# Value products in halves of 32 rows for four heads, and TensorE transposes for the first two batches, in a decay-attention and SiLU feed-forward kernel

## Chip, cores, metric

One core of a Trainium2 chip. The metric is device time in microseconds (us), the median of the fast runs. A span in a profile is that of one profiled run; it is 1.7 to 2.1 us shorter than the time of the same run. The engines are TensorE (PE; its weight loads are PEld), VectorE (DVE), ScalarE (ACT), GpSimd (POOL) and the sync engine (SP), which here only issues DMAs. The granted clock is the share of its full clock that TensorE was given; the DMA share is the mean busy share of the core's DMA engines.

## The reference

```python
def _attn_ref(q, k, v, f):                      # q, k, v: (8, 8, 576, 64), f: (8, 8, 576)
    scores = (1 / sqrt(64)) * (q @ k.T)
    cum = cumsum(log(clip(f, 1e-4, 1)))
    scores = scores + cum[..., :, None] - cum[..., None, :]      # causal: the rest is -1e9
    attn = softmax(scores)                                       # [the -max step is cut here]
    return attn @ v

x = attn_out.transpose(0, 2, 1, 3).reshape(4608, 512)            # the 8 heads of a token side by side
h = x @ w_in                                                     # w_in: 512 x 2048
return (h * sigmoid(h)) @ w_out                                  # w_out: 2048 x 512
```

All inputs are float32. The kernel computes in bf16 with float32 sums.

## The kernel before

The kernel takes two heads of one batch as a *unit* (4 units per batch, 32 in all). The decay factor of the row cancels between numerator and denominator, so only the key's factor `w` is left: it is multiplied into `v` (giving `vp`), and the denominator is the product of `w` with the same `u = exp(scores)`. The scores are computed transposed, keys on partitions, so q and k are needed with the head dimension on partitions. That is what the DMA transposes are for.

```python
def load_qk(n):                                # 128 rows of 64 floats: pieces of 256 bytes
    nc.sync.dma_start(out=t[:, :, i, :],
        in_=src[b, 2*p+i, 0:SM, :].rearrange("(c p) d -> p c d", p=P))
# ... cast_qk: GpSimd casts to bf16 ...
def transposes(n):                             # one DMA transpose per unit, on the sync queue
    nc.sync.dma_start_transpose(out=t, in_=qbf.pop(n))
# ... scores(n, c): four pieces per unit; ScalarE exp from PSUM to u; DVE masks ...

def den(qd):                                   # a quad = two units = four heads
    for kb, (q0, q1), j in ...:                # head j on partitions 32j .. 32j+31
        nc.tensor.matmul(dn[32*j : 32*j+32, q0:q1],
            lhsT=w_bf[:, kb, bh:bh+1].to_broadcast([P, 32]), rhs=u_part(...))
    nc.scalar.activation(out=rec, in_=dn, func=ACT.Copy)
def rec_part(qd, part):                        # half of the columns each
    nc.vector.reciprocal(out=rec[:, r], in_=rec[:, r])
    # after part 1: 8 DMAs copy each head's 32 rows twice, to the 64 partitions of its numerator
    nc.sync.dma_start(out=rb[i*D + 32*h : i*D + 32*h + 32, :], in_=rec[32*j : 32*j+32, :])
def num(n):                                    # a unit: two heads, 64 rows each
    nc.tensor.matmul(nm[i*D : (i+1)*D, q0:q1], lhsT=vp[:, kb, 2*p+i, :], rhs=u_part(...))
    nc.vector.tensor_tensor(out=xT[:, p, ...], in0=nm, in1=rb, op=ALU.mult)    # reads PSUM

def m1_chunk(g, fc):   # 4 matmuls 128x512 with w_in, tanh on ScalarE, gate on DVE -> gt
def m2_part(g, tb, part):  # 4 matmuls 128x512 with w_out; after the 4th part evict and store
def fill(n):           # n chunks of feed-forward, m1 or m2, from groups whose xT is finished
    ...
    if can1 and (not can2 or a - c <= 16 + (c % 2)): m1_chunk(...)
    else: m2_part(...)
def finished(n): ...   # counts the groups of 512 tokens whose xT is complete after unit n
# steady(n): scores in two pairs with fills between; den after each second unit,
# num of the pair one unit later
```

In before the sync queue stands up to 9.3 us at a copy with loads behind it. Two score-sized buffers of PSUM (`psc`) serve scores, denominators and numerators; four more (`pbig`) serve the feed-forward. There are 288 chunks of feed-forward.

The softmax here doesn't subtract the row's maximum and nothing guards it: scores larger than these inputs give would overflow.

## Time and profile before

| | before |
|---|---|
| time, median of 3 runs | 440.25 us (438.83 to 440.57) |
| span of the profiled run | 436.2 us |
| TensorE busy | 336.6 us (77%) |
| start of unit 8 (first of the third batch) | 106.4 us |
| from there to the end | 329.8 us |

Table of stretches of before. The columns are start:end and length; the busy time (instructions) of PE, PEld, DVE, ACT and POOL; the granted TensorE clock; the DMA share; and GB/s.

```profile
0.00:63.00 63.00, 17.63 (x215) 10.39 (x217) 18.83 (x35) 17.32 (x22) 20.16 (x42) 0.91 0.91 175
63.00:106.00 43.00, 25.21 (x225) 10.44 (x228) 23.42 (x40) 21.39 (x33) 12.93 (x19) 0.77 1.14 198
...
150.00:358.00 208.00, 187.02 (x1671) 88.32 (x1699) 138.45 (x220) 123.07 (x191) 53.55 (x84) 1.00 0.71 153
358.00:436.00 78.00, 73.85 (x365) 33.65 (x369) 25.18 (x37) 27.89 (x47) 0.00 (x0) 0.99 0.16 55
```

TensorE is busy for only 42.8 of the first 106 us, while the DMA share is at or above 0.9. The kernel has a bad start, and a steady part with about 10% of idle time.

Timeline of before in the start: start, length, engine, line, operation and count. In brackets is the idle time before the instruction and what ended it.

```profile
23.56 7.18 SPq L115 DMA_DIRECT2D vf_201<-in_v_dram  x1
30.79 4.43 SPq L115 DMA_DIRECT2D vf_202<-in_v_dram  x1
...
35.33 4.24 SPq L213 DMA_TRANSPOSE qkT<-qkb  x1
...
41.82 0.85 PE L238 MATMUL sc<-qkT 64*128 64x400 bf16 x6 [18.34 <-DMA qkT<-qkb]
...
43.31 5.04 SPq L303 DMA_DIRECT2D rb<-rec  x8
```

The sync queue is held up at value loads, and behind them stands the DMA transpose that the fourth unit's scores need. TensorE waits 18.34 us for it.

Who the sync queue waited for in before (total, times, longest):

```profile
SPq L380 <- ACT osb L379: 70.6, 14, 12.5
SPq L303 <- DVE rec L295: 53.7, 11, 9.3
```

The second line is the head of the queue standing still until a reciprocal is done. Every load and transpose behind it stands too. The table of TensorE's waits for 150 to 358 us in before shows what the steady part pays:

```profile
PE sc L238 <- DMA qkT<-qkb: 17.2, 12, 2.7
```

Three groups of the page of before (line, engine, operation, shape, count; busy us and mean ns; idle before and its releaser):

```profile
L325 DVE TENSOR_TENSOR xT<-nm,rb 128x576 bf16<-128x576 f32 x32 | 23.9, 756 | 52.3 <-DMA rb<-rec 33.7
...
L316 PE MATMUL nm<-u,vp 128*64 128x64 bf16 (+4 forms) x576 | 27.5, 252 | 3.3 <-DVE xT L325 2.4
...
L281 PE MATMUL dn<-u,w_bf 128*32 128x64 bf16 (+4 forms) x576 | 15.9, 256 | 1.3 <-DVE u L252 0.9
```

### The profile page before, as it was taken

How to read it: one execution, taken by the hardware profiler on the slowest of the kernel's cores; microseconds unless marked ns; L12 is line 12 of the kernel's file. 1: busy time of each engine (PE TensorE's matmuls, PEld its weight loads, DVE VectorE, ACT ScalarE, POOL GpSimd, SP SyncE). 2: the span in 40 equal slices, each digit the busy share in tenths (PEclk: the TensorE clock that was granted, in tenths of full speed). 3: DMA queues.
4: the chain of work that ended last, by engine and by line, in shares of the span. 5: the costliest groups of instructions: out<-in, count | busy, mean ns of one | idle time of the engine just before them, and what ended most of it. 6: DMA issues, size and time to landing. Idle time of an engine off the chain costs nothing.

```text
span 436.2 us, 7419 instructions
## 1 busy us (share of the span) xinstructions
PE 336.6 (77%) x2774; PEld 158.4 (36%) x2821; DVE 235.0 (54%) x375; ACT 213.2 (49%) x328; POOL 97.9 (22%) x163
## 2 busy tenths in 40 slices
PE   0511728608298899788988997898899899999996
PEld 0300403303143344344443443344444444444442
DVE  3230528616388438485847674776768472634310
ACT  3621208507266547465655555565667542543421
POOL 3424216403240144133213411350143000000000
PEclk9999859957789999999999999999999999999999
DMA  6999769899544987697598839894941413001011
GB/s 153 199 189 195 166 155 213 153 208 203 129 101 101 200 194 154 162 212 170 120 200 182 198 83 218 167 209 99 215 123 37 117 36 107 24 29 45 37 61 72
DMA packets 167092, 61.47 MB, mean 141 GB/s; under 512 B 154192, under 2 KB 158288, under 8 KB 167056
## 3 DMA queue, kind: packets, MB, share of 16 engines
q1 hardware_dynamic: 162832, 56.80, 61.2%
q0 software_dynamic: 4224, 4.19, 5.9%
q8 instruction: 22, 0.36, 0.4%
q14 instruction: 14, 0.11, 0.1%
HBM read 36.85 MB, written 9.44 MB: 106 GB/s over the span
## 4 chain that ended last, share of the span: by engine, by line
PE 42%; SPq 27%; DMA 18%; ACT 5%; issue 4%; DVE 2%; POOL 1%; POOLq 0%; DVEq 0%; ACTq 0%
PE hp L343 19%; PE po L370 18%; SPq L303 11%; DMA qkT<-qkb 11%; SPq L77 6%; SPq L115 5%; SPq L213 4%; DMA vf_199<-in_v_dram 3%; ACT u L245 3%; PE sc L238 3%; DMA rb<-rec 2%; PE nm L316 2%; ACT th L351 2%; PE dn L281 1%; DMA vf_3622<-in_v_dram 1%
## 5 line engine op out<-in xcount | busy, mean ns | idle before, releaser
L343 PE MATMUL hp<-xT,w_in_bf 128*128 128x512 bf16 x560 | 141.0, 390 | 10.4 <-DVE xT L325 8.0
L351 ACT ACTIVATE th<-hp 128x512 bf16<-128x512 f32 x144 | 85.4, 602 | 107.8 <-PE hp L343 107.7
L370 PE MATMUL po<-w_out_bf,gt 128*128 128x512 bf16 x545 | 132.5, 379 | 3.3 <-issue 2.5
L245 ACT ACTIVATE u<-sc 128x800 bf16<-128x800 f32 x128 | 100.0, 841 | 68.1 <-PE sc L238 67.8
L352 DVE SCALAR_TENSOR_TENSOR gt<-th,hp 128x512 bf16<-128x512 bf16 x144 | 94.6, 674 | 39.1 <-ACT th L351 38.3
L252 DVE TENSOR_TENSOR u<-u,mask 128x256 bf16<-128x256 bf16 x128 | 53.2, 431 | 74.2 <-ACT u L245 73.1
L238 PE MATMUL sc<-qkT 64*128 64x176 bf16 (+5 forms) x512 | 38.9, 269 | 70.2 <-DMA qkT<-qkb 63.5
L343 PEld LDWEIGHTS <-w_in_bf 128*128 128x128 bf16 x576 | 53.0, 99 | 73.4 <-issue 17.4
L370 PEld LDWEIGHTS <-gt 128*128 128x128 bf16 x576 | 53.8, 98 | 64.2 <-issue 2.6
L295 DVE RECIPROCAL rec<-rec 128x288 f32<-128x288 f32 x32 | 61.9, 1942 | 13.2 <-ACT rec L289 13.2
L99 POOL CAST qkb<-qf 128x512 bf16<-128x512 f32 x31 | 19.2, 619 | 198.1 <-DMA qkT<-qkb 122.9
L238 PEld LDWEIGHTS <-qkT 64*128 64x128 bf16 x512 | 20.1, 99 | 102.3 <-DMA qkT<-qkb 74.8
L325 DVE TENSOR_TENSOR xT<-nm,rb 128x576 bf16<-128x576 f32 x32 | 23.9, 756 | 52.3 <-DMA rb<-rec 33.7
L379 ACT ACTIVATE osb<-po 128x512 f32<-128x512 f32 x36 | 21.6, 601 | 25.3 <-PE po L370 24.8
L316 PE MATMUL nm<-u,vp 128*64 128x64 bf16 (+4 forms) x576 | 27.5, 252 | 3.3 <-DVE xT L325 2.4
L316 PEld LDWEIGHTS <-vp 128*64 128x64 bf16 x576 | 20.3, 115 | 14.9 <-issue 10.0
L99 POOL CAST qkb<-kf 128x512 bf16<-128x512 f32 x31 | 19.2, 619 | 2.4 <-DMA kf<-in_k_dram 2.3
L289 ACT ACTIVATE rec<-dn 128x576 f32<-128x576 f32 x16 | 10.4, 651 | 15.5 <-PE dn L281 13.4
L281 PE MATMUL dn<-u,w_bf 128*32 128x64 bf16 (+4 forms) x576 | 15.9, 256 | 1.3 <-DVE u L252 0.9
L281 PEld LDWEIGHTS <-w_bf 128*32 128x32 bf16 x576 | 10.6, 101 | 11.5 <-issue 7.1
L103 POOL CAST qkb<-qktf 128x128 bf16<-128x128 f32 x32 | 9.7, 303 | 5.5 <-DMA qktf<-in_k_dram 5.5
L257 DVE TENSOR_TENSOR u<-u,mask_t 128x128 bf16<-128x128 bf16 x32 | 7.6, 238 | 0.0
(69 smaller groups left out, 63.9 us busy)
## 6 DMA issues: line engine op xcount, KB each, us to landing
rb<-rec SPq DMA_DIRECT2D x128, 72.0 KB, 2.1
out_dram<-osb SPq DMA_DIRECT2D x36, 256.0 KB, 2.5
qf<-in_q_dram SPq DMA_DIRECT2D x64, 128.0 KB, 3.1
kf<-in_k_dram SPq DMA_DIRECT2D x64, 128.0 KB, 3.1
w_in_bf<-in_moe_w_in_dram POOLq DMA_DIRECT2D x4, 512.0 KB, 11.8
w_out_bf<-in_moe_w_out_dram POOLq DMA_DIRECT2D x4, 512.0 KB, 11.6
qktf<-in_q_dram SPq DMA_DIRECT2D x8, 128.0 KB, 3.2
qktf<-in_k_dram SPq DMA_DIRECT2D x8, 128.0 KB, 3.2
```

Source lines behind the costliest of these rows:

```text
L99: engs[i].tensor_copy(out=t2[:, c0 : c0 + NM, :], in_=t[:, :, :, :].rearrange("p c h d -> p c (h d)"),)
L238: nc.tensor.matmul(sc[:, i, lo - c * CW : hi - c * CW], lhsT=t[r, k_off(kb) : k_off(kb) + P], rhs=t[r, q0 : q0 + hi - lo], start=True, sto ...
L245: nc.scalar.activation(out=u[:, :, c * CW : (c + 1) * CW], in_=sc[:, :, 0:CW], func=ACT.Exp, scale=scale)
L252: nc.vector.tensor_tensor(out=x, in0=x, in1=mask[:, None, :].to_broadcast([P, 2, P]), op=ALU.mult)
L281: nc.tensor.matmul(dn[32 * j : 32 * j + 32, q0:q1], lhsT=w_bf[:, kb, bh : bh + 1].to_broadcast([P, 32]), rhs=u_part(n, i, kb, q0, q1), sta ...
L295: nc.vector.reciprocal(out=rec[:, r], in_=rec[:, r])
L303: nc.sync.dma_start(out=rb[i * D + 32 * h : i * D + 32 * h + 32, :], in_=rec[32 * j : 32 * j + 32, :],)
L316: nc.tensor.matmul(nm[i * D : (i + 1) * D, q0:q1], lhsT=vp[:, kb, 2 * p + i, :], rhs=u_part(n, i, kb, q0, q1), start=(kb == 0), stop=(kb = ...
L343: nc.tensor.matmul(hp[:, :], lhsT=w_in_bf[:, cc, fc * P : (fc + 1) * P], rhs=xT[:, cc, t0 : t0 + TG], start=(cc == 0), stop=(cc == NCC - 1),)
L351: nc.scalar.activation(out=th[:, :], in_=hp[:, :], func=ACT.Tanh, scale=0.5)
L352: nc.vector.scalar_tensor_tensor(out=gt[:, fc, :], in0=th[:, :], scalar=1.0, in1=hp[:, :], op0=ALU.add, op1=ALU.mult,)
L370: nc.tensor.matmul(po[:, :], lhsT=gt[:, fc, tb * P : (tb + 1) * P], rhs=w_out_bf[:, fc, :], start=(fc == 0), stop=(fc == NFC - 1),)
```

## The change

The intent has three parts.

- Products are made as two passes over four heads, 32 of the 64 value rows each, so a numerator lies on the same partitions as the denominator. No copies of the reciprocal are needed, and ScalarE can evict numerators before the reciprocal is there. The features of `xT` come out in another order, so the rows of `w_in` are loaded permuted to match.
- The first two batches are transposed by matmuls with the identity, so the start needs no DMA transpose, and their q and k are read in rows of 1 KB. The permuted token order is undone by a strided PSUM write.
- The schedule is written anew: all first loads up front, GpSimd for the multiplies, 16 feed-forward chunks in batch 1, and from the third batch on 7 and 11 fills in turn (9 per unit).

The diff, cut to its core:

```diff
 def load_qk(n):
+    if n < NPT:                                            # NPT = 8 units
+        nc.sync.dma_start(out=t[:, i*NM*D : (i+1)*NM*D],
+                          in_=s.rearrange("(p c) d -> p (c d)", p=P))
 def transposes(n):
+    if n >= NPT: ... DMA transpose as before; return
+    for x0 in (0, NM + 1):                                 # q, then k
+        for c in range(NM):
+            nc.tensor.matmul(tp[:, :, c], lhsT=src[:, x0 + c, :], rhs=ident_bf)
+        nc.vector.tensor_copy(out=t[:, x0 : x0 + NM, :], in_=tp)
+        # ... the tails likewise, between q and k ...
-        for m in range(2): ... 8 DMAs rb <- rec ...
-def num(n): ... 64 rows per head, DVE multiply from PSUM ...
+def quad(qd, what):                                        # what: half 0, half 1, or 2 = w
+    nc.tensor.matmul(dn[HD*j : HD*(j+1), q0:q1],
+        lhsT=w or vbf[b][:, kb, h, what*HD : (what+1)*HD], rhs=u_part(...))
+def num(qd, e):
+    nc.scalar.activation(out=nm, in_=quad(qd, e)[:, 0:S], func=ACT.Copy)
+def divide(qd, e, eng):
+    eng.tensor_tensor(out=xT[:, (2*qd % NP) + e, ...], in0=nm, in1=recs[qd], op=ALU.mult)
 # load_w_in: moe_w_in.rearrange("(g j e r) f -> g e j r f", j=4, e=2)
 # third batch on, in unit n:
+    scores(n, 0); scores(n, 1); fill(2)
+    # load_qk(n + 4); cast_qk(n + 2); transposes(n + 2); ...
+    fill(2); scores(n, 2); scores(n, 3); fill(3)
+    if n % 2 == 1:
+        fill(1); den(m); rec_part(m, 0); num(m, 0); num(m, 1); fill(1); rec_part(m, 1)
+        divide(m, 0, nc.gpsimd); divide(m, 1, nc.gpsimd); fill(2); finished(n)
```

More of the change, by code (lines that the diff above doesn't have):

```diff
@@ L43 @@
     NX = 2 * NM + 1
+    NPT = 2 * NP
+    NQ = NU // 2
+    HD = D // 2
     assert D == 64 and S == 576 and DM == H * D and NP == NCC
@@ L55 @@
     recp = ctx.enter_context(tc.tile_pool(name="recp", bufs=2))
-    rbp = ctx.enter_context(tc.tile_pool(name="rbp", bufs=4))
+    nmp = ctx.enter_context(tc.tile_pool(name="nmp", bufs=4))
     tpool = ctx.enter_context(tc.tile_pool(name="tpool", bufs=3))
@@ L74, in load_qk @@
         for name, src in (("qf", q), ("kf", k)):
-            t = stage.tile([P, NM, 2, D], FP32, name=name, tag=name, bufs=5)
+            t = stage.tile([P, 2 * NM * D], FP32, name=name, tag=name, bufs=4)
             for i in range(2):
-                nc.sync.dma_start(
-                    out=t[:, :, i, :],
-                    in_=src[b, 2 * p + i, 0:SM, :].rearrange("(c p) d -> p c d", p=P),
-                )
+                s = src[b, 2 * p + i, 0:SM, :]
+                if n < NPT:
+                    nc.sync.dma_start(
+                        out=t[:, i * NM * D : (i + 1) * NM * D],
+                        in_=s.rearrange("(p c) d -> p (c d)", p=P),
+                    )
+                else:
+                    nc.sync.dma_start(
+                        out=t[:, :].rearrange("p (c h d) -> p c h d", h=2, d=D)[:, :, i, :],
+                        in_=s.rearrange("(c p) d -> p c d", p=P),
+                    )
             ts.append(t)
@@ L98, in cast_qk @@
             c0 = i * (NM + 1)
-            engs[i].tensor_copy(
-                out=t2[:, c0 : c0 + NM, :],
-                in_=t[:, :, :, :].rearrange("p c h d -> p c (h d)"),
-            )
+            dst = t2[:, c0 : c0 + NM, :]
+            if n < NPT:
+                engs[i].tensor_copy(
+                    out=dst.rearrange("p c (h d) -> p c h d", h=2),
+                    in_=t[:, :].rearrange("p (h c d) -> p c h d", h=2, d=D),
+                )
+            else:
+                engs[i].tensor_copy(out=dst, in_=t[:, :].rearrange("p (c x) -> p c x", c=NM))
         nc.gpsimd.tensor_copy(
@@ L123 @@
     load_tails(0)
-    load_qk(1)
+    for n in range(1, NP):
+        load_qk(n)
+    for c in range(NM + 1):
+        load_v(0, c)
     ident_bf = const.tile([P, P], BF16, name="ident_bf")
@@ L140, with load_w_in @@
     w_bf = const.tile([P, NM + 1, BH], BF16, name="w_bf")
-    WQ = 4
-    def load_w_in(i):
-        c0, c1 = i * DFF // WQ, (i + 1) * DFF // WQ
-        nc.gpsimd.dma_start(
-            out=w_in_bf[:, :, c0:c1],
-            in_=moe_w_in[:, c0:c1].rearrange("(cc p) f -> p cc f", p=P),
-        )
+    w_in_v = moe_w_in.rearrange("(g j e r) f -> g e j r f", g=NCC // 2, j=4, e=2)
+    def load_w_in(i):
+        c0, c1 = i * DFF // 2, (i + 1) * DFF // 2
+        for cc in range(NCC):
+            nc.gpsimd.dma_start(
+                out=w_in_bf[:, cc, c0:c1], in_=w_in_v[cc // 2, cc % 2, :, :, c0:c1]
+            )
+    WQ = 4
     def load_w_out(i):
@@ L179, with weights, convert_v @@
     nc.vector.tensor_copy(out=wexp[:, S : S + ST], in_=wexp[:, SM:S])
-    wps = pbig.tile([P, NM + 1, BH], FP32, name="wps", tag="big")
-    for c in range(NM + 1):
-        nc.tensor.transpose(wps[:, c, :], wexp[:, c * P : (c + 1) * P], ident_f[:, :])
-    nc.vector.tensor_copy(out=w_bf[:, :, :], in_=wps[:, :, :])
-    setup_pool.__exit__(None, None, None)
-    gpool = ctx.enter_context(tc.tile_pool(name="gpool", bufs=2))
+    def weights():
+        wps = pbig.tile([P, NM + 1, BH], FP32, name="wps", tag="big")
+        for c in range(NM + 1):
+            nc.tensor.transpose(wps[:, c, :], wexp[:, c * P : (c + 1) * P], ident_f[:, :])
+        nc.vector.tensor_copy(out=w_bf[:, :, :], in_=wps[:, :, :])
     qkT: dict[int, bass.AP] = {}
     us: dict[int, tuple] = {}
-    def convert_v(b, c):
+    def convert_v(b, c, eng=nc.gpsimd):
         if b not in vbf:
@@ L197, in convert_v @@
             r = slice(ST, P)
-            nc.gpsimd.memset(vp[0:ST, NM, :, :], 0.0)
+            eng.memset(vp[0:ST, NM, :, :], 0.0)
         n = r.stop - r.start
-        nc.gpsimd.tensor_tensor(
+        eng.tensor_tensor(
             out=vp[r, c, :, :],
@@ L211, in transposes @@
     def transposes(n):
+        src = qbf.pop(n)
         t = qktp.tile([P, NX, P], BF16, name="qkT", tag="qkT")
-        nc.sync.dma_start_transpose(
-            out=t[:, :, :], in_=qbf.pop(n)[:, :, :].rearrange("p x c -> p (x c)")
-        )
         qkT[n] = t[:, :, :].rearrange("p x c -> p (x c)")
+        if n >= NPT:
+            nc.sync.dma_start_transpose(
+                out=t[:, :, :], in_=src[:, :, :].rearrange("p x c -> p (x c)")
+            )
+            return
+        for x0 in (0, NM + 1):
+            tp = pbig.tile([P, P, NM], FP32, name="tp", tag="big")
+            for c in range(NM):
+                nc.tensor.matmul(
+                    tp[:, :, c],
+                    lhsT=src[:, x0 + c, :],
+                    rhs=ident_bf[:, :],
+                    start=True,
+                    stop=True,
+                )
+            nc.vector.tensor_copy(
+                out=t[:, x0 : x0 + NM, :].rearrange("p x c -> p (x c)"),
+                in_=tp[:, :, :].rearrange("p t c -> p (t c)"),
+            )
+            if x0 == 0:
+                tt = pbig.tile([P, 8 * P], BF16, name="tt", tag="big")
+                nc.tensor.transpose(tt[:, 0:P], src[:, NM, :], ident_bf[:, :])
+                nc.vector.tensor_copy(out=t[:, NM, :], in_=tt[:, 0:P])
     UO = [0]
@@ L270 @@
     recs: dict[int, bass.AP] = {}
-    dens: dict[int, tuple] = {}
-    def den(qd):
+    def quad(qd, what):
+        b = qd * 2 // NP
         dn = psc.tile([P, 1024], FP32, name="dn", tag="sc")
@@ L278, in den @@
                     n, i = 2 * qd + j // 2, j % 2
-                    b, p = divmod(n, NP)
-                    bh = b * H + 2 * p + i
+                    h = 2 * (n % NP) + i
+                    if what == 2:
+                        w = w_bf[:, kb, b * H + h : b * H + h + 1].to_broadcast([P, HD])
+                    else:
+                        w = vbf[b][:, kb, h, what * HD : (what + 1) * HD]
                     nc.tensor.matmul(
-                        dn[32 * j : 32 * j + 32, q0:q1],
-                        lhsT=w_bf[:, kb, bh : bh + 1].to_broadcast([P, 32]),
+                        dn[HD * j : HD * (j + 1), q0:q1],
+                        lhsT=w,
                         rhs=u_part(n, i, kb, q0, q1),
@@ L287, in den @@
                     )
+        return dn
+    def den(qd):
+        dn = quad(qd, 2)
         rec = recp.tile([P, S], FP32, name="rec", tag="rec")
         nc.scalar.activation(out=rec[:, :], in_=dn[:, 0:S], func=ACT.Copy)
-        dens[qd] = rec
+        recs[qd] = rec
     def rec_part(qd, part):
-        rec = dens[qd]
         r = slice(part * S // 2, (part + 1) * S // 2)
-        nc.vector.reciprocal(out=rec[:, r], in_=rec[:, r])
-        if part == 0:
-            return
-        for m in range(2):
-            rb = rbp.tile([P, S], FP32, name="rb", tag="rb")
-            for i in range(2):
-                j = 2 * m + i
-                for h in range(2):
-                    nc.sync.dma_start(
-                        out=rb[i * D + 32 * h : i * D + 32 * h + 32, :],
-                        in_=rec[32 * j : 32 * j + 32, :],
-                    )
-            recs[2 * qd + m] = rb
-    def num(n):
-        b, p = divmod(n, NP)
-        vp = vbf[b]
-        nm = psc.tile([P, 1024], FP32, name="nm", tag="sc")
-        for kb in range(NM + 1):
-            for q0, q1 in q_parts(kb):
-                for i in range(2):
-                    nc.tensor.matmul(
-                        nm[i * D : (i + 1) * D, q0:q1],
-                        lhsT=vp[:, kb, 2 * p + i, :],
-                        rhs=u_part(n, i, kb, q0, q1),
-                        start=(kb == 0),
-                        stop=(kb == NM or (kb == NM - 1 and q0 < SM)),
-                    )
-        us.pop(n)
-        rb = recs.pop(n)
-        nc.vector.tensor_tensor(
-            out=xT[:, p, b * S : (b + 1) * S], in0=nm[:, 0:S], in1=rb[:, :], op=ALU.mult
+        nc.vector.reciprocal(out=recs[qd][:, r], in_=recs[qd][:, r])
+    nms: dict[tuple, bass.AP] = {}
+    def num(qd, e):
+        dn = quad(qd, e)
+        nm = nmp.tile([P, S], FP32, name="nm", tag="nm")
+        nc.scalar.activation(out=nm[:, :], in_=dn[:, 0:S], func=ACT.Copy)
+        nms[qd, e] = nm
+    def divide(qd, e, eng):
+        b = qd * 2 // NP
+        eng.tensor_tensor(
+            out=xT[:, (2 * qd % NP) + e, b * S : (b + 1) * S],
+            in0=nms.pop((qd, e))[:, :],
+            in1=recs[qd][:, :],
+            op=ALU.mult,
         )
@@ L382 @@
     done = {"m1": 0, "m2": 0}
-    ready = {"g": 0}
+    ready = {"g": 0, "m2": False}
     def fill(n):
@@ L388, in fill @@
             can1 = a < 16 * ready["g"] and a < 16 * (c // 16) + 32
-            can2 = c < 16 * (a // 16) and a >= 32
+            can2 = c < 16 * (a // 16) and ready["m2"]
             if not can1 and not can2:
@@ L402, in finished @@
             ready["g"] += 1
+    POOLS = (nc.gpsimd, nc.gpsimd)
     transposes(0)
-    for n in range(1, NP):
-        load_qk(n + 1)
-        cast_qk(n, (nc.gpsimd, nc.gpsimd))
-        if n == NP - 1:
-            for c in range(NM + 1):
-                load_v(0, c)
-        transposes(n)
-    for i in range(WQ):
-        load_w_in(i)
-    for c in range(NM + 1):
-        convert_v(0, c)
-    load_tails(1)
-    load_qk(NP + 1)
-    def steady(n):
+    weights()
+    setup_pool.__exit__(None, None, None)
@@ new lines @@
+    gpool = ctx.enter_context(tc.tile_pool(name="gpool", bufs=2))
+    for n in range(NP):
+        scores(n, 0)
+        scores(n, 1)
+        if n + 1 < NP:
+            cast_qk(n + 1, POOLS)
+            transposes(n + 1)
+        scores(n, 2)
+        scores(n, 3)
+        if n == 1:
+            den(0)
+            load_qk(NP)
+            load_tails(1)
+            load_qk(NP + 1)
+        if n == 2:
+            rec_part(0, 0)
+            rec_part(0, 1)
+            for c in range(NM + 1):
+                convert_v(0, c, nc.gpsimd if c < 2 else nc.vector)
+            load_w_in(0)
+            load_w_in(1)
@@ new lines @@
+    den(1)
+    rec_part(1, 0)
+    rec_part(1, 1)
+    for m in range(2):
+        for e in range(2):
+            num(m, e)
+            divide(m, e, nc.gpsimd if m == 0 else nc.vector)
+    finished(NP - 1)
+    load_qk(NP + 2)
+    load_qk(NP + 3)
+    for c in range(NM + 1):
+        load_v(1, c)
+    cast_qk(NP, POOLS)
+    fill(3)
+    transposes(NP)
+    fill(1)
+    for n in range(NP, 2 * NP):
+        scores(n, 0)
+        scores(n, 1)
+        if n + 1 < 2 * NP:
+            cast_qk(n + 1, POOLS)
+            transposes(n + 1)
+        load_qk(n + NP)
+        if n == NP:
+            load_tails(2)
+        fill(1)
+        scores(n, 2)
+        scores(n, 3)
+        fill(1)
+        if n % 2 == 1:
+            m = n // 2
+            if n == NP + 1:
+                for c in range(NM + 1):
+                    convert_v(1, c)
+            den(m)
+            rec_part(m, 0)
+            rec_part(m, 1)
+            for e in range(2):
+                num(m, e)
+                divide(m, e, nc.gpsimd)
+            fill(2)
+            if n == NP + 1:
+                for i in range(WQ):
+                    load_w_out(i)
@@ L421, in steady @@
+    finished(2 * NP - 1)
+    for c in range(NM + 1):
+        load_v(2, c)
+    for n in (2 * NP, 2 * NP + 1):
+        cast_qk(n, POOLS)
+        transposes(n)
+    ready["m2"] = True
+    for n in range(2 * NP, NU):
         b, p = divmod(n, NP)
@@ L423, in steady @@
         scores(n, 1)
-        fill(1)
-        if n + 2 < NU and n + 2 >= NP:
-            cast_qk(n + 2, (nc.gpsimd, nc.gpsimd))
-        if n + 5 < NU and n >= NP:
-            load_qk(n + 5)
-        if b + 1 < B:
-            if p == 0 and b > 0:
-                load_tails(b + 1)
-            if p == 2 and b > 0:
-                for c in range(NM + 1):
-                    load_v(b + 1, c)
-        if b > 0:
-            if p == 0:
-                for c in range(2):
-                    convert_v(b, c)
-            if p == 1:
-                for c in range(2, NM + 1):
-                    convert_v(b, c)
@@ L442, in steady @@
-        if n == NP + 2:
-            for i in range(WQ):
-                load_w_out(i)
-        fill(1 if n >= 2 * NP else 0)
+        fill(2)
+        if n + 4 < NU:
+            load_qk(n + 4)
+        if n + 2 < NU:
+            cast_qk(n + 2, POOLS)
+            transposes(n + 2)
+        if p == 0 and b + 1 < B:
+            load_tails(b + 1)
+        if p < 2:
+            for c in range(2 * p, 2 + 3 * p):
+                convert_v(b, c)
+        if p == 1 and b + 1 < B:
+            for c in range(NM + 1):
+                load_v(b + 1, c)
@@ L446, in steady @@
+        fill(2)
         scores(n, 2)
         scores(n, 3)
-        fill(4 - n % 2 if n >= 2 * NP else 1)
+        fill(3)
         if n % 2 == 1:
-            den(n // 2)
-            rec_part(n // 2, 0)
-            fill(2 if n >= 2 * NP else 1)
-            rec_part(n // 2, 1)
-            fill(1 if n >= 2 * NP else 0)
-            if n == NP - 1:
-                for m in range(NP):
-                    num(m)
-                finished(n)
-                fill(4)
-        elif n >= 2 and n != 2 and n != NP:
-            num(n - 2)
-            num(n - 1)
-            fill(2 if n >= 2 * NP else 1)
-            finished(n - 1)
@@ L465, in steady @@
-        if n + 2 < NU and n + 2 >= NP:
-            transposes(n + 2)
-        if n + 5 < NU and 1 <= n < NP:
-            load_qk(n + 5)
-        if n == NP - 1:
-            for c in range(NM + 1):
-                load_v(1, c)
-    for n in range(NU):
-        steady(n)
-    fill(12)
-    num(NU - 2)
-    fill(2)
-    num(NU - 1)
-    finished(NU - 1)
+            m = n // 2
+            fill(1)
+            den(m)
+            rec_part(m, 0)
+            for e in range(2):
+                num(m, e)
@@ L480 @@
+            fill(1)
+            rec_part(m, 1)
+            for e in range(2):
+                divide(m, e, nc.gpsimd)
+            fill(2)
+            finished(n)
     while fill(1):
```

## The prediction

> **What bounds it now.** By the page, the span is 436.2 us, TensorE busy 336.6 (77%). At the tail's rate (8 matmuls of 128x512 in 1.73 us, chain of waits) the 1,152 feed-forward matmuls need 249 us; scores, denominators and value products add about 33 + 14 + 26: some 320 us. The other 115 are start and waits. By the table of stretches TensorE is busy 17.6 of the first 63 us, 25.2 of 63-106 (granted clock 0.77), 187 of 208 in 150-358, 74 of 78 in the tail.
>
> The start is lost to the sync queue and its DMAs. In the timeline the queue stands at value loads from 20.7 to 35 us (one lands after 13.4), a DMA transpose then takes 4.2 us to issue, and scores wait 18.3; later 8 copies rb<-rec per pair of units (5.0 us of issue), and the queue waits 53.7 us in total for the reciprocal before them. Feed-forward starts in earnest at 63 us; unit 8 (third batch) at 106.4. In 150-358 TensorE waits 17-24 us for DMA transposes.
>
> **What changes.**
> - Removed: 128 copies (9.4 MB, some 75 us of queue issue, and the wait before them).
> - TensorE stays level: four heads of 32 columns fill 128 columns as two of 64 did [...]. The trace agrees: a denominator pass (36 matmuls) takes 0.87 us, a pair of units' products 1.59. Two passes: 1.74; +2.4 us over 16.
> - ScalarE: 32 evictions of about 0.65 us, +21. DVE: most multiplies (0.76 us) leave for GpSimd, an estimated 1.2-1.3 us each from its 1.04-1.1 for 128x512. Neither becomes the limit.
> - First 8 units: 8 DMA transposes go; per unit TensorE gains 9 small matmuls (about 0.6 us warm), DVE 1.7 us of evictions (estimated from 0.49 us for 128x320 from PSUM). q/k rows come 1 KB at a time instead of 256 B[...].
> - From the third batch 9 fills per unit, not 8.
>
> **Sum.** Batch 0 at 4.4 us per unit from 10.5 us, then two reciprocals of 3.9: feed-forward starts near 39 us. Batch 1 is limited by DVE, 7 us a unit plus a cold start: 35. Then a new bubble of about 8: reciprocal, GpSimd divide, cast, DMA transpose (3.9) in series before unit 8, which starts near 82, 24 us earlier, with 16 of 288 chunks done, as before. The rest: 272 x 0.865 = 235; 12 pairs x 5.1 = 61; waits 8; batches 5-7 ask for more chunks than are ready, exposing the divide chain, 9; end 4. Together 317, against 330 before. Span 399; my stretches are a little high.
>
> **Predicted: 395 us, range 378 to 414.** Faster by over 2%: 0.94; within 2%: 0.04; slower: 0.02.
>
> **What would show it.** No rb copies; the sync queue no longer waiting on the reciprocal; feed-forward near 39 us, unit 8 near 82; transposes near 0 in TensorE's steady waits; 0.87 us for each half's pass; a TensorE gap before unit 8; pairs of units near 21.3 us with 18 chunks.
>
> **What would make it wrong.** Strided PSUM writes of TensorE running slowly; GpSimd divides well over 1.3 us beside DVE; weights landing after 45 us; the granted clock near 0.75 through batch 1; three adjacent passes stalling on two PSUM buffers.

The sum stands as it was made: 39 + 35 + 8 = 82 us for unit 8, then 317, together 399, less 4 for stretches "a little high": 395. On the size of rows the page of before has this: 154,192 of 167,092 packets are under 512 B. That their size costs time was not shown. The 0.6 us for nine matmuls was the estimate; nine times a quarter of the 0.216 us that a 128x512 matmul took in the tail of before (1.73 us for 8) would be 0.49 us.

## The result, and the profile after

| | before | after |
|---|---|---|
| time, median | 440.41 us (4 runs) | 415.14 us (414.69 to 416.79, 4 runs) |
| ratio of the fast runs | | 0.9421 (95%: 0.9356 to 0.9487) |
| TensorE busy, span of the profiled run | 336.6 of 436.2 us | 353.4 of 415.0 us |
| start of unit 8 | 106.4 us | 86.8 us |
| from there to the end | 329.8 us | 328.2 us |

A ratio is the mean time of one kernel's fast runs over that of the other's in the same rounds. It is not quite the ratio of the medians.

The kernel is 25 us faster. The forecast of 395 us was 20 us too low, and the result lies 1.1 us above the range. The gain came from the start: unit 8 begins 19.6 us earlier, and everything after it takes as long as before. (These are the two profiled runs, whose spans are 21.2 us apart; the medians are 25.3 us apart.)

Table of stretches of after:

```profile
0.00:63.00 63.00, 36.91 (x531) 23.52 (x534) 46.51 (x82) 35.37 (x49) 33.34 (x56) 0.91 0.89 180
63.00:106.00 43.00, 32.28 (x312) 14.98 (x319) 19.51 (x37) 20.77 (x33) 15.66 (x24) 0.81 0.86 152
...
150.00:358.00 208.00, 190.15 (x1968) 87.92 (x1986) 122.22 (x183) 126.97 (x198) 72.36 (x92) 0.95 0.49 108
358.00:415.00 57.00, 52.72 (x239) 23.79 (x242) 20.64 (x30) 22.64 (x38) 0.00 (x0) 0.98 0.10 38
```

TensorE is busy twice as long in the first 63 us. In 150 to 358 us its busy time hardly rises, although DMA is down from 0.71 to 0.49, and its clock is 0.95 instead of 1.00.

TensorE's waits in after, over the whole run:

```profile
PE hp L377 <- POOL xT L356: 15.6, 12, 3.9
PE sc L280 <- DMA qkT<-qkb: 8.9, 1, 8.9
PE tp L244 <- POOL qkb L112: 7.3, 1, 7.3
```

And the sync queue's largest:

```profile
SPq L414 <- ACT osb L413: 161.9, 27, 31.4
```

The waits for DMA transposes are gone but for one, and the sync queue no longer waits for the reciprocal; its wait for output tiles keeps nobody waiting. In their place stands a new wait: the feed-forward's first product waits for GpSimd's multiplies.

Groups of the page of after:

```profile
L356 POOL TENSOR_TENSOR xT<-nm,rec 128x576 bf16<-128x576 f32 x30 | 42.0, 1418 | 201.5 <-DVE u L294 100.1
...
L327 PE MATMUL dn<-u,vp 128*32 128x64 bf16 (+4 forms) x1152 | 29.7, 251 | 1.7
```

The halves cost TensorE what was expected: 29.7 us against 27.5. A multiply on GpSimd took 1.42 us (mean of 30), where I had put 1.2 to 1.3; the two on DVE took 0.775 and 1.015 us for the same shape.

Timeline of after in batch 1:

```profile
53.63 3.76 DVE L344 RECIPROCAL rec<-rec 128x288 f32<-128x288 f32 x2 [0.29 <-ACT rec L339]
...
57.56 2.80 POOL L356 TENSOR_TENSOR xT<-nm,rec 128x576 bf16<-128x576 f32 x2 [8.11 <-DVE rec L344]
...
60.31 3.10 POOL L174 DMA_DIRECT2D w_out_bf<-in_moe_w_out_dram  x4
63.38 0.65 POOL L112 CAST qkb<-qf 128x512 bf16<-128x512 f32 x1
...
64.09 1.04 PE L244 MATMUL tp<-ident_bf,qkb 128*128 128x128 bf16 x4 [7.29 <-POOL qkb L112]
...
79.14 2.75 POOL L356 TENSOR_TENSOR xT<-nm,rec 128x576 bf16<-128x576 f32 x2 [14.33 <-DVE rec L344]
81.84 0.60 POOL L117 CAST qkb<-qf 128x512 bf16<-128x512 f32 x1
...
83.26 2.92 SPq L237 DMA_TRANSPOSE qkT<-qkb  x2
...
86.80 0.85 PE L280 MATMUL sc<-qkT 64*128 64x400 bf16 x6 [8.85 <-DMA qkT<-qkb]
```

Read it upwards from each wait of TensorE. At 64.09 TensorE waits for a cast on GpSimd. The cast stands in GpSimd's queue behind four DMA issues and two multiplies, and the multiplies stand there until DVE has the reciprocal. GpSimd itself was idle for 8.11 us. At 86.80 it is the same chain with a DMA transpose at its end.

Timeline of after at the end of batch 2 (unit 12's scores began at 130.38):

```profile
126.86 3.76 DVE L344 RECIPROCAL rec<-rec 128x288 f32<-128x288 f32 x2 [1.98 <-ACT rec L339]
...
130.77 2.81 POOL L356 TENSOR_TENSOR xT<-nm,rec 128x576 bf16<-128x576 f32 x2 [13.41 <-DVE rec L344]
...
132.23 0.38 PE L377 MATMUL hp<-xT,w_in_bf 128*128 128x512 bf16 x1 [0.79 <-POOL xT L356]
...
133.63 4.65 PE L377 MATMUL hp<-xT,w_in_bf 128*128 128x512 bf16 x13 [1.03 <-POOL xT L356]
```

The waits are 0.79 and 1.03 us, one for each multiply. Then 13 matmuls take 4.65 us. At another batch end, after the same two waits, TensorE's timeline of after has:

```profile
222.66 2.96 PE L377 MATMUL hp<-xT,w_in_bf 128*128 128x512 bf16 x13 [1.03 <-POOL xT L356]
```

The same work took 1.69 us less. The table of stretches of after, by pairs of units, shows why (first pair of a batch, second pair, and the first pair that belongs to 222.66):

```profile
130.40:154.60 24.20, 21.98 (x212) 9.91 (x216) 14.07 (x24) 15.09 (x24) 11.06 (x14) 0.93 0.83 171
154.60:175.00 20.40, 20.00 (x212) 9.52 (x216) 12.65 (x18) 12.64 (x19) 5.62 (x8) 1.00 0.39 96
...
219.40:242.10 22.70, 20.53 (x210) 9.46 (x212) 16.96 (x28) 16.73 (x27) 11.21 (x14) 1.00 0.82 149
```

A pair with 18 chunks needs 20.40 us. The first pair of a batch takes 22.7 us where the clock stayed at 1.00 and 24.2 us where it fell. So a batch end costs 2.3 us, of which the two waits are 1.8, and, most times, 1.5 us more of half clock. At the last two batches the waits are 2.88 + 0.77 and 3.93 + 0.77 us.

The working theory from here: (a) the start gained because DMA transposes left it; (b) two gaps in batch 1 come from the order of GpSimd's queue; (c) at every batch end the chain reciprocal, multiply, multiply lies open, plus a clock penalty; and these, with the size of (b), are what the prediction missed. The rivals: the stalls come from DMA traffic, from GpSimd's speed, from running out of ready chunks, or from the larger number of fills.

### The profile page after: what moved, and what is told of

The parts are those of the page before. It is cut to its first block, busy times and chain, and to the rows that moved or that the text cites. A ratio compares the mean times of both kernels' runs of the same rounds, so it can differ in the third digit from the quotient of the medians.

```text
span 415.0 us, 8554 instructions
## 1 busy us (share of the span) xinstructions
PE 353.4 (85%) x3427; PEld 169.2 (41%) x3469; DVE 236.5 (57%) x373; ACT 234.3 (56%) x360; POOL 138.0 (33%) x193
## 4 chain that ended last, share of the span: by engine, by line
PE 67%; DVE 8%; issue 6%; DMA 5%; ACT 4%; POOL 4%; SPq 3%; another core or an unknown queue 1%; POOLq 1%; ACTq 0%
PE hp L377 29%; PE po L404 27%; PE dn L327 6%; PE sc L280 5%; DVE rec L344 4%; POOL xT L356 3%; ACT rec L339 2%; DMA qf<-in_q_dram 2%; DMA vf<-in_v_dram 2%; ACT u L287 1%; DVE u L294 1%; SPq L88 1%; DVE qkT L251 1%; DMA qkT<-qkb 1%; SPq L130 1%
## 5 line engine op out<-in xcount | busy, mean ns | idle before, releaser
L377 PE MATMUL hp<-xT,w_in_bf 128*128 128x512 bf16 x549 | 149.0, 407 | 20.7 <-POOL xT L356 15.6
L356 POOL TENSOR_TENSOR xT<-nm,rec 128x576 bf16<-128x576 f32 x30 | 42.0, 1418 | 201.5 <-DVE u L294 100.1
L294 DVE TENSOR_TENSOR u<-u,mask 128x256 bf16<-128x256 bf16 x128 | 56.6, 450 | 63.2 <-ACT u L287 62.3
L280 PE MATMUL sc<-qkT 64*128 64x176 bf16 (+5 forms) x512 | 35.2, 254 | 14.5 <-DMA qkT<-qkb 8.9
L221 POOL TENSOR_TENSOR vp<-vf,w_bf 128x512 bf16<-128x512 f32 (+1 forms) x37 | 38.1, 1044 | 2.7 <-DMA vf<-in_v_dram 1.8
L327 PE MATMUL dn<-u,vp 128*32 128x64 bf16 (+4 forms) x1152 | 29.7, 251 | 1.7
L327 PEld LDWEIGHTS <-vp 128*32 128x32 bf16 x1152 | 22.0, 101 | 7.9 <-issue 3.3
L351 ACT ACTIVATE nm<-dn 128x576 f32<-128x576 f32 x32 | 20.8, 650 | 7.1 <-PE dn L327 7.1
L244 PE MATMUL tp<-ident_bf,qkb 128*128 128x128 bf16 x64 | 10.9, 353 | 14.1 <-POOL qkb L112 7.3
L117 POOL CAST qkb<-qf 128x512 bf16<-128x512 f32 x24 | 14.8, 616 | 2.3 <-DMA qkT<-qkb 2.3
```

What stands on the lines that cost most here:

```text
L221: eng.tensor_tensor(out=vp[r, c, :, :], in0=vst[b][c][r, :, :], in1=w_bf[r, c, b * H : (b + 1) * H, None].to_broadcast([n, H, D]), op=ALU. ...
L280: nc.tensor.matmul(sc[:, i, lo - c * CW : hi - c * CW], lhsT=t[r, k_off(kb) : k_off(kb) + P], rhs=t[r, q0 : q0 + hi - lo], start=True, sto ...
L294: nc.vector.tensor_tensor(out=x, in0=x, in1=mask[:, None, :].to_broadcast([P, 2, P]), op=ALU.mult)
L327: nc.tensor.matmul(dn[HD * j : HD * (j + 1), q0:q1], lhsT=w, rhs=u_part(n, i, kb, q0, q1), start=(kb == 0), stop=(kb == NM or (kb == NM - ...
L356: eng.tensor_tensor(out=xT[:, (2 * qd % NP) + e, b * S : (b + 1) * S], in0=nms.pop((qd, e))[:, :], in1=recs[qd][:, :], op=ALU.mult,)
L377: nc.tensor.matmul(hp[:, :], lhsT=w_in_bf[:, cc, fc * P : (fc + 1) * P], rhs=xT[:, cc, t0 : t0 + TG], start=(cc == 0), stop=(cc == NCC - 1),)
```

## The experiments

Twelve kernels were run, all with correct results, all at 3 rounds. The ratio is to before in the same rounds. "Unit 8" is the time of its first score matmul in the profiled run, and "rest" is what is left of that run's span from there. Runs of different calls were made against before on different chips, so small differences between them are read from the ratios.

| run | what | median us | ratio (95%) | unit 8 | rest |
|---|---|---|---|---|---|
| after | | 415.14 | 0.942 (0.936 to 0.949) | 86.8 | 328.2 |
| w1_warm | dummy matmuls at batch ends | 408.35 | 0.928 (0.923 to 0.933) | 88.4 | 318.1 |
| s1_split | one multiply on DVE | 406.89 | 0.925 (0.919 to 0.930) | 85.8 | 317.8 |
| c1_casts | casts ahead of multiplies, batch 1 | 402.27 | 0.914 (0.909 to 0.919) | 73.8 | 327.8 |
| n0_dmat | TensorE transposes undone | 447.18 | 1.017 (1.011 to 1.023) | 119.4 | 326.0 |
| d8_defer | later count of a batch, 8 fills | 389.72 | 0.887 (0.883 to 0.891) | 88.2 | 299.8 |
| r1_rows | rows of 256 B, TensorE transposes kept | 417.09 | 0.949 (0.942 to 0.956) | 89.3 | 328.3 |
| k1_copies | copies put back, unused | 416.91 | 0.949 (0.942 to 0.956) | 87.1 | 327.6 |
| b1_all | mended parts together | 372.26 | 0.846 (0.841 to 0.851) | 73.5 | 296.8 |
| bt_only | before + TensorE transposes | 428.41 | 0.972 (0.966 to 0.978) | 96.1 | 333.2 |
| f8_fills | 8 fills only | 407.63 | 0.925 (0.920 to 0.930) | 89.0 | 317.8 |
| d9_defer | later count only | 394.72 | 0.897 (0.893 to 0.902) | 87.3 | 306.3 |
| h1_pairs | b1_all, halves undone | 438.60 | 0.997 (0.992 to 1.003) | 99.2 | 336.7 |

### w1_warm: is the slow stretch after the wait the clock?

```diff
         scores(n, 1)
+        if p == 0 and b > 2:
+            warm(9 if b < 7 else 18)    # dummy 128x512 matmuls into a spare PSUM tile
         fill(2)
```

with `warm(22)` before the closing fills.

> Kernel after, with dummy 128x512 matmuls (9 at the ends of batches 2 to 5, 18 and 22 at the last two) put on TensorE just before the first feed-forward chunk that waits for the new batch. They feed nothing; the divides come no sooner. Theory (each batch end costs the wait of about 1.8 us, or 3.7 to 4.7 at the last two, AND a spell at half clock that costs 1.5 to 2 us more): the 13 matmuls after the wait take about 2.8 us as in the one warm case of after, not 4.65, the granted clock from 130 us on is 1.0, and the time falls 7 to 10 us, to 405 to 408. Rival (the slow matmuls after the wait come from memory traffic of GpSimd and DVE, or the wait alone is the cost): 415 within 2, or a little over.

Measured: 408.35 us, just above the forecast. TensorE's timeline of w1_warm at the same batch end:

```profile
131.74 2.12 PE L437 MATMUL dm<-w_in_bf,ident_bf 128*128 128x512 bf16 x9
133.69 3.83 PE L377 MATMUL hp<-xT,w_in_bf 128*128 128x512 bf16 x16
```

The 16 matmuls take 3.83 us, and the clock over 130 to 175 us is 1.00. The multiplies came no sooner, and from 130 to 175 us the DMA share (0.60, in after 0.62) and DVE's busy time (29.1 us, in after 27.1) were about what they had been, so the traffic is not the cause. Doing useless work in place of waiting gains 6.8 us.

### s1_split: is it GpSimd's two multiplies in a row?

```diff
-            for e in range(2):
-                divide(m, e, nc.gpsimd)
+            divide(m, 0, nc.vector)
+            divide(m, 1, nc.gpsimd)
```

> Kernel after, but from the third batch on the two multiplies of a quad run side by side, the first on DVE and the second on GpSimd, instead of both on GpSimd one after the other (2 x 1.40 us). Theory (the batch end waits for the chain reciprocal, multiply, multiply): the wait ends 1.4 us sooner at each of six batch ends, 0.8 us or less is left at batches 2 to 5, most of these no longer fall to half clock: 415 falls by 8 to 16 us, to 399 to 407. Rival (GpSimd's multiplies are off the path and the reciprocal on DVE sets it): within 3 us of 415.

Measured: 406.89 us, 8.3 us less, at the edge of the forecast. The mean clock is 0.958 against 0.937, so not every fall of the clock is avoided; waits of up to 3.3 us are left. The multiplies are one link of the chain, not the whole of it. At batches 2 to 5 one wait of 0.88 us is left of the 1.82, so the split saves 0.9 us there and not 1.4. Timeline of s1_split, the same batch end:

```profile
129.12 1.98 POOL L356 TENSOR_TENSOR xT<-nm,rec 128x576 bf16<-128x576 f32 x1 [14.20 <-DVE rec L344]
```

Begun together with DVE's, GpSimd's multiply took 1.98 us here; two in a row took 1.40 each in after.

### c1_casts: is it the order of GpSimd's queue in batch 1?

```diff
             convert_v(1, c)
+        cast_qk(n + 2, POOLS)           # n = 5; w_out is issued here as well
+    else:                               # n = 7
+        for x in (n + 1, n + 2): cast_qk(x, POOLS); transposes(x)
     den(m); rec_part(m, 0); rec_part(m, 1)
-    # load_w_out after the multiplies; cast_qk and transposes of units 8, 9 after batch 1
```

> Kernel after, but in the second batch the casts for the next units (and the issue of the w_out load) stand in GpSimd's queue ahead of the multiplies that wait for the reciprocal, and the DMA transposes of units 8 and 9 with them. Theory (GpSimd's in-order queue makes the TensorE gaps of 7.3 us at 57 and of 8.9 us before unit 8): both gaps go but for about 3 us of wait for the batch's last multiply; unit 8 starts near 73 to 76 instead of 86.8 and the time falls 10 to 14 us, to 401 to 405. Rival (the gaps are set by the q/k loads or by DVE): unit 8 moves by less than 4 us.

Measured: 402.27 us, and unit 8 at 73.8 us. TensorE's timeline of c1_casts:

```profile
73.82 0.52 PE L280 MATMUL sc<-qkT 64*128 64x400 bf16 x6 [1.53 <-DMA qkT<-qkb]
```

The gap of 8.85 us is now 1.53, and that of 7.29 us no longer shows among TensorE's waits. Not one instruction was removed. In after, casts stood behind a multiply that waited, with GpSimd idle for 8.11 and 14.33 us; the first of them starts at 63.38 us there and at 50.06 us in c1_casts, so it was not data that it lacked: GpSimd kept to the order of its queue.

### n0_dmat: what are the TensorE transposes worth?

```diff
-    NPT = 2 * NP
+    NPT = 0
```

> Kernel after with the TensorE transposes undone: all batches go through DMA transposes and q/k rows are read 256 B at a time again; everything else as in after. If the gain of the start (unit 8 at 86.8 instead of 106.4) is from the transposes on TensorE: unit 8 at 100 to 110, time 425 to 440. If it is from the loads issued early and from the missing copies of the reciprocal: unit 8 below 93, time at most 421.

Measured: 447.18 us, more than forecast and 1.7% above before. TensorE's timeline of n0_dmat has two of its five waits for DMA transposes (62.1 us in all):

```profile
53.94 0.85 PE L280 MATMUL sc<-qkT 64*128 64x400 bf16 x6 [22.10 <-DMA qkT<-qkb]
...
119.42 0.85 PE L280 MATMUL sc<-qkT 64*128 64x400 bf16 x6 [8.67 <-DMA qkT<-qkb]
```

Without its transposes the changed kernel has no gain at all. With all loads up front, the DMA transposes stand behind more loads than in before: the first leaves the sync queue at 17.1 us, in before at 8.6. Issuing one took the queue 1.3 to 4.2 us in before. The edit also takes back the rows of 1 KB, which r1_rows tests.

### d8_defer: the batch ends

```diff
-            fill(2); finished(n)                        # after the multiplies of a quad
+            fill(2)
...
         fill(2)
+        finished(n - 1)                                 # next unit, after its first four fills
         scores(n, 2); scores(n, 3)
-        fill(3)
+        fill(2)                                         # 8 per unit on average
...
+    fill(4); finished(NU - 1)                           # after the last unit
```

> Kernel after, but from the third batch on a batch counts as finished only after the first four fills of the next batch (so the feed-forward's second product, which is ready, runs while the multiplies end), and a unit is given 8 fills on average instead of 9, so that a batch never runs out of ready chunks. Theory (the first pair of units of each batch is 2.3 to 7.3 us longer than the second, 20.40 us, by the wait for the multiplies and the half clock after it): these 28 us over six batch ends go, granted clock 1.0 from 100 us on, time 389 to 394. Rival (the wait moves elsewhere: to two PSUM buffers, to DVE, or to the tail): 405 or more.

Measured: 389.72 us, as forecast. The table of stretches of d8_defer:

```profile
130.00:340.00 210.00, 207.93 (x2143) 97.76 (x2142) 142.97 (x214) 142.95 (x226) 82.54 (x105) 1.00 0.55 123
```

TensorE is busy 99% of the time at full clock. GpSimd's multiplies are the same as in after (1.42 us each there), and the wait for them, 15.6 us in after, is not among TensorE's largest waits in d8_defer, listed down to 0.9 us.

### f8_fills and d9_defer: which of the two edits did it?

f8_fills has only the `fill(3)` to `fill(2)` line, d9_defer only the later `finished`.

> Kernel after with 8 fills per unit instead of 9 and nothing else (a batch still counts as finished at once). Theory (9 fills use up the ready chunks, so that in the last two batches all of the reciprocal and multiply chain lies open; with 8 each batch end costs about the 3.7 us of the earlier ones): the two batch ends that cost 7.3 us each cost about 3.7, time 406 to 411. Rival (running out of chunks costs nothing as the work comes later anyway): 415 within 2.

> Kernel after with the later count of a finished batch alone, at 9 fills. Theory (there are ready chunks of the second product to put in only at the ends of batches 2 to 4; later ends have none, and the wait stays): the three ends that cost 3.8 + 3.6 + 2.3 us are gone, the later ones stay, time 402 to 408. If the deferral alone does all of the 25 us of the joint run: 392 or less.

Measured: 407.63 us for f8_fills, as forecast, and 394.72 us for d9_defer, better than forecast. So the later count brings 20 of the 25 us even at 9 fills. I had held that at the ends of batches 5 to 7 no chunk is ready to put in, so the wait must stay. TensorE's timeline of d9_defer at such an end shows what happens in place of it:

```profile
253.89 0.35 PE L280 MATMUL sc<-qkT 64*128 64x224 bf16 x4 [1.01 <-ACT u L287]
```

The fills find nothing and return, and the next scores run at once, with a wait of 1.01 us. The missing chunks run later, in the tail. With the later count, running out of ready chunks is cheap, though not free: d8_defer, which does not run out, is 5 us faster, and at the end of batch 7 d9_defer still waits 1.34 + 0.98 us for the multiplies. With the early count it opens the whole chain, and f8_fills, by not running out, gained 7.5 us (its longest wait for a multiply is 1.3 us, in after 3.9). Dearer than either is to take a chunk that is counted as ready but whose inputs are still being made.

### r1_rows: do the rows of 1 KB matter?

```diff
-                if n < NPT:            # load and cast in the old order, 256 B pieces
+                if n < 0:
-            tp = pbig.tile([P, P, NM], ...)    # matmuls write tp[:, :, c], stride 16 B
+            tp = pbig.tile([P, NM, P], ...)    # matmuls write tp[:, c, :]
```

> Kernel after, with TensorE transposes in the first two batches, but q/k rows read 256 B at a time in the old order (the transposes then write PSUM without stride). Theory (the start gains because DMA transposes leave the sync queue; the rows' size is a small part): unit 8 within 4 us of 86.8 and time 415 to 420. Rival (the start is limited by bytes in small packets, so the 1 KB rows matter most): time 425 or more. If the strided PSUM write cost anything, the transposes' matmuls (353 ns mean, 0.60 us for 4 warm) would be shorter here.

Measured: 417.09 us, interval overlapping that of after. Unit 8 is 2.5 us later in the profiled run. The rows are a small part, if any: no cost of 256 B is resolved here (ratio 0.949, 0.942 to 0.956, against 0.942, 0.936 to 0.949). The strided PSUM write does cost something. TensorE's timelines have, at full clock in batch 1, four transposes of after (first line) and of r1_rows (second line):

```profile
42.43 0.61 PE L244 MATMUL tp<-ident_bf,qkb 128*128 128x128 bf16 x4
```

```profile
43.63 0.40 PE L244 MATMUL tp<-ident_bf,qkb 128*128 128x128 bf16 x4
```

The mean of the 64 fell from 353 to 277 ns, which was the test that I had set; all of them together took 10.9 us in after and 8.1 in r1_rows. (The median is 314 ns in both, but by chance: that is a strided write at full clock and an unstrided one at half clock.) As this gain of up to 2.8 us works against any cost of the short rows, r1_rows shows only that the two together change nothing resolved.

### k1_copies: did the copies cost time in the steady part?

```diff
     nc.vector.reciprocal(out=rec[:, r], in_=rec[:, r])
+    if part == 0 or qd < NP: return
+    for m in range(2): ... 8 DMAs rb <- rec, as in before; rb is never read
```

> Kernel after with the 8 copies of the reciprocal per quad put back into the sync queue from the third batch on (their target is never read; the result stays right). Theory (in the steady part the copies were not what cost time in itself, but their place ahead of the DMA transposes; here the transposes are issued two units ahead): within 3 us of 415, no waits of TensorE for DMA transposes over 1 us. Rival (removing the copies is what took the 17 to 24 us of waits for transposes away): these waits return, 425 or more.

Measured: 416.91 us, no difference resolved. The sync queue of k1_copies does wait for the reciprocal again:

```profile
SPq L354 <- DVE rec L346: 55.5, 12, 16.0
```

and no TensorE wait for a transpose came with it beyond the 8.9 us before unit 8 that after has too. In the new order the transposes for unit n + 2 are issued in the first half of unit n, ahead of the copies of that unit, so the copies are not on the path. In before they come right behind the copies and are late: one is issued at 199.84 us, and the scores at 203.12 have waited 1.03 us for it.

### bt_only: one half of the change alone

This is before with `load_qk`, the casts and `transposes` of the new kernel for the first two batches, and nothing else.

> Kernel before with one half of the change alone: the first two batches' q/k read in rows of 1 KB and transposed on TensorE; products of 64 rows, copies of the reciprocal and the order of before kept. Theory (the start's transposes are the whole gain of the change, the 32-row halves on their own gain nothing): unit 8 at 85 to 95 instead of 106, the rest near 330 as before, time 410 to 425. Rival (the halves and the missing copies carry a good part of the 25 us): 428 or more.

Measured: 428.41 us, at the value that I had given to the rival. Unit 8 is at 96.1 us, a little over my range, and the rest is about as in before. The transposes alone bring 12.6 us, half of the change's gain. All else without them (n0_dmat) loses 6 us. The gains of the parts do not add up. A flaw of this kernel makes its number a poor measure of the transposes alone: the order of before puts unit 4's transposes ahead of unit 3's scores, and on TensorE that blocks the scores (a wait of 12.9 us for a cast that stood behind the value conversion). TensorE's timeline of bt_only:

```profile
37.93 1.03 PE L234 MATMUL tp<-ident_bf,qkb 128*128 128x128 bf16 x4 [12.86 <-POOL qkb L108]
```

### b1_all: the mended parts together

c1_casts, d8_defer and s1_split in one kernel, and batch 1 too is counted as finished later.

> All of the mended parts together: casts ahead of the multiplies in the second batch, 8 fills per unit, a batch counted as finished after the next one's first four fills (the third batch too), one of the two multiplies on DVE. Theory: gains add, 402.3 of the casts less 22 to 26 of the deferral less about 3 for the wait at unit 8: 372 to 380. If the DVE, with the multiplies and closer packing, becomes the limit: 385 or more.

Measured: 372.26 us, as forecast, 15% below before and 10% below after. The table of stretches of b1_all from unit 8 on:

```profile
73.50:358.00 284.50, 282.84 (x2730) 132.24 (x2731) 183.37 (x287) 184.74 (x293) 91.95 (x116) 1.00 0.55 121
```

TensorE is busy 99.4% of 284 us at full clock. The stretch from unit 8 to the end takes 296.8 us.

### h1_pairs: the halves undone in the mended kernel

b1_all with 64-row products per pair, the copies of the reciprocal, DVE multiplies from PSUM, and `w_in` not permuted. The products come after the next unit's first four fills.

> The joint kernel (372 us) with the 32-row halves undone: products of 64 rows for two heads, the reciprocal brought to their partitions by 8 copies per quad, the multiply on DVE straight from PSUM, weights not permuted; products come one unit later as in before. Theory (the halves themselves are worth little; what counts is TensorE transposes at the start and the order of work): 370 to 382, most of the loss at the start, where the copies queue behind loads. Rival (the halves are needed for the gain): 388 or more.

Measured: 438.60 us. My theory was wrong here by almost 60 us. Two lines of the waits of h1_pairs, of TensorE and of the sync queue:

```profile
PE sc L280 <- DVE xT L376: 29.2, 13, 9.1
```

```profile
SPq L353 <- DVE rec L345: 81.9, 13, 11.3
```

The scores wait for the multiply. A 64-row numerator stays in one of the two PSUM buffers until its copied reciprocal has landed, and the scores need that buffer. In the halves' form ScalarE evicts the numerator without any reciprocal. These waits are 29.2 of the 66 us between the two kernels; the rest was not taken apart (unit 8 comes 25.7 us later, and the mean clock is 0.933 against 0.982). So what the copies' own time does not explain (k1_copies: none), the tie between PSUM and the multiply explains in part. The halves are one way to undo it. Whether ScalarE could evict 64-row numerators as early, and how much of the 66 us another order of the 64-row form could win back, was not tried; so it is not shown that the halves themselves are needed.

## Why the prediction was wrong

Point by point.

- **TensorE level, 0.87 us for each half's pass, ScalarE and DVE not the limit:** right. The halves took 29.7 us against 27.5, ScalarE's 32 evictions 20.8 us.
- **No copies, no wait of the sync queue for the reciprocal, no steady waits for transposes:** right. But the 17 us of waits that went between 150 and 358 us were replaced by 13.8 us of waits for GpSimd's multiplies there (15.6 over the whole run).
- **"9 small matmuls (about 0.6 us warm)", an estimate:** too low, because of the strided PSUM write: nine take 1.1 us in after (42.43 to 43.53 us) and 0.7 in r1_rows without the stride (43.63 to 44.31). "Strided PSUM writes of TensorE running slowly" was on the list of what would make the forecast wrong. It came true, but r1_rows, which is without it, is no faster; it is not what failed.
- **"Feed-forward starts near 39 us":** it started at 35.3, better than said.
- **"Batch 1 ... 35. Then a new bubble of about 8":** the second term was right (8.85 us). The first was too small: from 35.3 us the batch and the bubble took 51.5 us instead of 43. The step left out is a first bubble of 7.29 us, the same chain of reciprocal, multiply and cast after the first quad of batch 1, with the w_out issue in it. c1_casts took both bubbles away and moved unit 8 to 73.8 us. Unit 8 was at 86.8 us, 5 us later than "near 82".
- **"The rest: 272 x 0.865 = 235; 12 pairs x 5.1 = 61":** right in size. Work and its end take 296.8 us in b1_all, where almost nothing waits; the two terms and the 4 of the end make 300. A pair with 18 chunks took 20.40 us, where 21.3 was said.
- **"waits 8; batches 5-7 ask for more chunks than are ready, exposing the divide chain, 9":** this step failed, in mechanism and in size. The chain is exposed at every batch end, not at three, because `fill` takes the first product of a group that is counted as finished while its multiplies run. And such a pair of gaps, 0.79 + 1.03 us, can be followed by half clock: 0.50 for 3.41 us on three of four occasions. Against the 20.40 us of a pair, the five first pairs from 130 us on cost 3.8 + 3.7 + 2.3 + 3.8 + 7.3 = 20.9 us, and the last batch end had 4.7 us of waits and another slow stretch. With the slow start of unit 8's batch (a granted clock of 0.53 from 87 to 93 us; 43.6 us for its two pairs instead of 40.8) the terms that I had put at 8 + 9 are about 28. d8_defer recovers 25 us. w1_warm, which leaves the multiplies late and only keeps the clock up, gains 6.8 of it. The cause that I gave, running out of chunks, is the smaller part: f8_fills, which ends it and nothing else, gains 7.5 us, and d9_defer, which leaves it and counts later, gains 20.
- The guess that my stretches were "a little high", which took 399 down to 395, had no ground in a number and went the wrong way.

The total: 4 us better at the first feed-forward, 8.5 us worse in batch 1 with its bubbles, 11 us worse after unit 8, and the 4 us of the last guess. That makes 20 us.

The clock deserves a note. In after the granted clock is 0.50 for 3.41 us each time, from 133.66, 178.03 and 266.78 us. Before each of these stretches stand two waits of 0.79 to 0.80 and 1.02 to 1.03 us with one matmul between them, at 130, 176 and 264 us, and the 13 matmuls after the waits take 4.55 to 4.65 us. The same two waits at 221 us had no such stretch after them: 13 matmuls in 2.96 us. Why not there is not shown. One wait alone, of 0.88 us, was not enough at the end of batch 2 in s1_split (13 matmuls in 2.97 us). With 9 dummy matmuls (2.12 us) in the wait, 18 and 22 at the last two batch ends, the clock of w1_warm was 1.00 from 130 to 358 us, where that of after was 0.95, and the time 6.8 us less.

## What to carry to other kernels

A count of "ready" work should say that its inputs exist, not that the instructions that make them have been issued; putting the count off by four chunks of other work gained 20 us by itself, where the whole change had gained 25. Where an engine takes its work in the written order, as GpSimd did here with 8.11 us of idle time, look at what stands in front of the instruction that others wait for, not at how busy the engine is: GpSimd was busy 33% and still held TensorE up for 16 us at the start. When a wait of TensorE is costed, the slow matmuls after it belong to it as well: here 1.69 us more for 13 matmuls, after 1.82 us of waits.
